# Block 0's attention in two halves, the first FFN tiles begun on half 0, and q's second half loaded last

## The chip, the cores and the metric

The kernel runs on one core of one Trainium2 chip. The time is the device time of that core for one launch, in microseconds. Every run told here was in the fast state. The kernel before took 1116.95 us (median of 3 runs, 1115.8 to 1117.8) when the prediction was made.

## The reference, cut to what matters

```python
kv  = np.einsum('bhsd,bhse->bhde', k, v)         # 8 batches, 8 heads, 576 tokens, width 64
out = np.einsum('bhsd,bhde->bhse', q, kv)
rms = np.sqrt(np.mean(out * out, axis=-1, keepdims=True) + 1e-06)
x   = (out / rms * g_norm)                       # -> (4608, 512), fp32
g   = x @ w_gate                                 # 512 x 1536, float64 in the input
silu = g * (1 / (1 + exp(-g)))
out = (silu * (x @ w_val)) @ w_out               # 1536 x 512
```

Linear attention without a mask, a norm per head, then a gated FFN. The weights arrive as float64 and are rounded to float32 on the core.

## The kernel before: the parts that matter

The 4608 tokens go in nine blocks of 512. Block 0 has no work of another block to hide behind: its attention comes first, on an empty TensorE. Its FFN is "plain", with 12 tiles of 128 columns for the gate and 12 for the value, each of four matmuls of 128x512. The eight later blocks are a different algorithm, and keep TensorE full (119.88 us busy of the 120 from 150 to 270 us).

```python
def all(self):                        # block 0's attention
    for i in range(2):
        self.turn_q(i)                # transposes of q; copies on ScalarE and VectorE
    self.kv(range(NS))                # 192 matmuls of 64x64, wait for k and v
    self.product(0)                   # q @ kv of 256 tokens; squares (ScalarE), sums (VectorE)
    self.product(1, (b_psum, c_psum))
    self.root(0, 2)                   # 1/sqrt of both halves: 11 small VectorE instructions
    for i in range(2):
        self.scale(i)                 # two 128x512 multiplies on VectorE
        self.turn_x(i)                # 8 transposes on TensorE, 2 copies with gain on ScalarE
    return self.scaled
...
def plain_up(self, f):                # one tile of gate and value
    ps = []
    for pool, w in ((b_psum, wg), (c_psum, wv)):
        ps.append(pool.tile([P, BLK], F32, name=pool.name[0]))
        for i in range(NS):
            nc.tensor.matmul(ps[-1], lhsT=w[f // 2][:, i, ...], rhs=self.att.x[:, i, :], ...)
    g = ring("s", BLK)
    nc.scalar.activation(out=g, in_=ps[0], func=ACT.Silu)
    mul(nc.vector, self.h[:, f, :], g, ps[1])
...
blocks[0].load(room)                  # q, then k and v
weights(1)                            # load five weight pieces, round piece 0
scaled = blocks[0].all()
...
        for f in range(NF):
            with tc.issue_after(scaled.ins):
                weights(2 * (f + 2))  # round the pieces that tile f + 1 needs
            ffn.plain_up(f)
        ...
        for j in range(NP):
            t2(wv[j][:, 0:2], wv[j][:, 2:4], wg[j][:, 0:2])   # sums of weights for later blocks
```

`issue_after(x)` queues what stands under it behind x. Rounding one weight piece takes two passes on ScalarE (lines L141 and L143) and four instructions on VectorE (L144, L149, L150, L154).

## Time and profile before

| | before |
|---|---|
| time when predicted, median of 3 | 1116.95 us |
| span of the profiled run | 1113.7 us |
| TensorE busy | 1092.4 us |
| last of the four kv groups starts / ends | 16.66 / 18.21 us |
| first transposes of the normed x start (called T here) | 29.98 us |
| down projection starts | 116.77 us |

Two dates carry the whole argument: T, where TensorE ends its long idle, and the start of the down projection, where block 0's up stage ends. From there to the end of the span it is 996.9 us. The difference between the two dates, 86.79 us, is called the stretch below. In a timeline line the first number is the start, the second the length; the bracket gives the idle time before it and what ended it.

### The profile page before, as it was taken

To read this page: it belongs to the slowest core of one execution; us is meant where nothing else is said; L and a number is where in the kernel's file an instruction comes from. 1 tells how busy PE (TensorE), PEld (TensorE's weight loads), DVE (VectorE), ACT (ScalarE), POOL (GpSimd) and SP (SyncE) were. 2 spreads that over 40 slices of the span, in tenths; PEclk is the share of its full clock that TensorE was granted. 3 is DMA by queue.
4 is the path that set the end of the run, shared out by engine and by line. 5 is a ranking of instruction groups with operands and counts; after the bars stand their busy time and mean duration, and the time that the engine had idled before them with its cause. 6 is when DMAs were issued, how large, how long until landed. Compare 5 with 4: busy or idle time off the path is not lost.

```text
span 1113.7 us, 15512 instructions
## 1 busy us (share of the span) xinstructions
PE 1092.4 (98%) x6528; PEld 901.2 (81%) x6528; DVE 444.2 (40%) x759; ACT 272.4 (24%) x460; POOL 401.0 (36%) x320
## 2 busy tenths in 40 slices
PE   5999999999999999999999999999999999999998
PEld 4444548888888888888888888888888888888887
DVE  2999333126322551156113721263124621561221
ACT  2655112222122212222222122221222122222210
POOL 0021003452344334442444334532543345424550
PEclk9999999999999999999999999999999999999999
DMA  9677410310122010300040012101200100000001
GB/s 273 194 221 186 109 54 19 86 39 1 39 51 51 23 38 26 77 23 26 13 102 23 1 39 61 42 22 38 52 19 1 38 1 1 1 30 10 1 1 38
DMA packets 70245, 57.62 MB, mean 52 GB/s; under 512 B 39456, under 2 KB 64032, under 8 KB 70176
## 3 DMA queue, kind: packets, MB, share of 16 engines
q1 hardware_dynamic: 70112, 56.63, 18.9%
q8 instruction: 51, 0.84, 0.3%
q14 instruction: 18, 0.15, 0.0%
q0 software_dynamic: 64, 0.00, 0.0%
HBM read 47.19 MB, written 9.44 MB: 51 GB/s over the span
## 4 chain that ended last, share of the span: by engine, by line
PE 89%; DVE 1%; DMA 0%; issue 0%
PE b L383 45%; PE c L383 22%; PE a L383 11%; PE b L559 4%; PE m L237 2%; PE m L271 2%; PE m L315 1%; PE m L251 1%; PE b L546 0%; PE c L546 0%; DVE u L150 0%; DMA ld<-in_v_dram 0%; DVE wo L154 0%; DVE g L149 0%; PE a L271 0%; DVE u L144 0%
## 5 line engine op out<-in xcount | busy, mean ns | idle before, releaser
L110 POOL TENSOR_TENSOR t<-wg,wv 128x512 f32<-128x512 f32 x96 | 123.9, 1292 | 182.5 <-PE b L383 92.0
L110 POOL TENSOR_TENSOR t<-wv 128x512 f32<-128x512 f32 x48 | 63.9, 1331 | 323.9 <-PE c L383 117.8
L109 DVE TENSOR_TENSOR s<-h 128x256 f32<-128x256 f32 x48 | 20.4, 425 | 307.8 <-POOL h L111 307.8
L110 POOL TENSOR_TENSOR t<-wo 128x512 f32<-128x512 f32 x72 | 91.4, 1269 | 121.5 <-PE c L383 70.6
L383 PE MATMUL b<-x,t 128*128 128x256 f32 x384 | 91.3, 381 | 0.8
L383 PE MATMUL b<-x,wg 128*128 128x256 f32 x384 | 92.0, 382 | 0.0
L109 DVE TENSOR_TENSOR u<-c,u 128x512 f32<-128x512 f32 x96 | 65.9, 687 | 63.1 <-ACT u L425 63.1
L383 PE MATMUL a<-x,wg 128*128 128x256 f32 x384 | 90.9, 379 | 0.0
L383 PE MATMUL c<-xs,t 128*128 128x256 f32 x384 | 90.8, 379 | 0.0
L383 PE MATMUL b<-xs,t 128*128 128x256 f32 x384 | 90.8, 379 | 0.0
L383 PE MATMUL c<-xs,wv 128*128 128x256 f32 x384 | 90.7, 379 | 0.0
L383 PE MATMUL b<-x,wv 128*128 128x256 f32 x384 | 90.7, 379 | 0.0
L383 PE MATMUL b<-t,h 128*128 128x256 f32 x384 | 86.3, 381 | 0.0
L383 PE MATMUL b<-wo,h 128*128 128x256 f32 x384 | 85.8, 379 | 0.0
L398 ACT COPY u<-b 128x512 f32<-128x512 f32 x56 | 32.8, 586 | 214.2 <-PE b L383 214.2
L383 PEld LDWEIGHTS b<-x,t 128*128 128x128 f32 x384 | 72.3, 190 | 12.0 <-issue 2.5
L383 PEld LDWEIGHTS c<-xs,t 128*128 128x128 f32 x384 | 72.9, 190 | 10.3 <-issue 0.4
L383 PEld LDWEIGHTS b<-xs,t 128*128 128x128 f32 x384 | 72.9, 190 | 10.1 <-issue 0.3
L383 PEld LDWEIGHTS b<-x,wv 128*128 128x128 f32 x384 | 73.0, 190 | 9.9
L383 PEld LDWEIGHTS c<-xs,wv 128*128 128x128 f32 x384 | 73.0, 190 | 9.9
L383 PEld LDWEIGHTS a<-x,wg 128*128 128x128 f32 x384 | 73.0, 190 | 9.9
L111 POOL TENSOR_TENSOR h<-s,u 128x512 f32<-128x512 f32 x48 | 60.9, 1269 | 54.7 <-DVE u L109 54.7
(88 smaller groups left out, 1534.5 us busy)
## 6 DMA issues: line engine op xcount, KB each, us to landing
out_dram<-o SPq DMA_DIRECT2D x18, 512.0 KB, 2.8
ld<-in_q_dram SPq DMA_DIRECT2D x32, 256.0 KB, 5.0
ld<-in_k_dram SPq DMA_DIRECT2D x28, 288.0 KB, 4.6
ld<-in_v_dram SPq DMA_DIRECT2D x28, 288.0 KB, 4.1
ld<-in_moe_w_gate_dram SPq DMA_DIRECT2D x12, 512.0 KB, 4.8
ld<-in_moe_w_val_dram SPq DMA_DIRECT2D x12, 512.0 KB, 5.2
ld<-in_moe_w_out_dram SPq DMA_DIRECT2D x12, 512.0 KB, 4.1
h<-in_k_dram SPq DMA_DIRECT2D x4, 288.0 KB, 6.2
```

What stands on the lines that cost most here:

```text
L109: add = lambda e, o, a, b: e.tensor_tensor(out=o, in0=a, in1=b, op=OP.add)
L110: sub = lambda e, o, a, b: e.tensor_tensor(out=o, in0=a, in1=b, op=OP.subtract)
L111: mul = lambda e, o, a, b: e.tensor_tensor(out=o, in0=a, in1=b, op=OP.mult)
L237: nc.tensor.matmul(self.kv_ps[u * D : (u + 1) * D, j, :], lhsT=self.k[j][:, u, c, :], rhs=self.v[j][:, u, c, :], start=(c == 0), stop=(c = ...
L251: nc.tensor.transpose(ps[:, j], self.q[t][:, j], ident)
L271: nc.tensor.matmul(self.ps[i][u][p : p + D, t, j, :], lhsT=self.qt[rows, 2 * i + t, j, p : p + D], rhs=kvs[b % 3][rows, j, :], start=True, ...
L315: nc.tensor.transpose(ps[:, e, t], xt[:, t, j + e], ident)
L383: nc.tensor.matmul(self.ps[name][:, e], lhsT=lhsT, rhs=rhs, start=first and (e, i) == (0, 0), stop=i == self.steps - 1, skip_group_check=True,
L398: nc.scalar.copy(out=self.u2, in_=self.ps["b"])
L559: nc.tensor.matmul(ps, lhsT=self.h[:, f, P * t : P * (t + 1)], rhs=wo[:, f, :], start=(f == 0), stop=(f == NF - 1),)
```

## The change

The intent is to give TensorE half 0's FFN matmuls while half 1 is still being normed, and to have k and v land sooner by loading q's second half after them. The diff, cut to its core:

```diff
 def load(self, room=None):
-    self.load_q()
+    self.load_q(0)
+    if not room:
+        self.load_q(1)
     ... # k and v
+    if room:                          # block 0 only
+        self.load_q(1)
...
-def all(self):
-    for i in range(2):
-        self.turn_q(i)
-    self.kv(range(NS))
-    self.product(0)
-    self.product(1, (b_psum, c_psum))
-    self.root(0, 2)
-    for i in range(2):
-        self.scale(i)
-        self.turn_x(i)
+def first(self):
+    self.turn_q(0)
+    self.kv(range(NS))
+    self.half(0)                      # product, root and scaling of half 0
+    self.turn_q(1, (b_psum, c_psum))
+    self.product(1, (m_psum, a_psum))
+    self.turn_x(0)
+def second(self):
+    self.root(1)
+    self.scale(1)
+    self.turn_x(1)
...
-def plain_up(self, f):
+def plain_up(self, f, halves=(0, 1)): # may do 256 of the 512 columns
...
-scaled = blocks[0].all()
+scaled = blocks[0].first()
...
+            with tc.issue_after(scaled.ins):
+                weights(2)
+            ffn.plain_up(0, (0,))
+            scaled = blocks[0].second()
             for f in range(NF):
                 with tc.issue_after(scaled.ins):
                     weights(2 * (f + 2))
-                ffn.plain_up(f)
+                if f == 1:
+                    ffn.plain_up(1, (0,))
+                    ffn.plain_up(0, (1,))
+                ffn.plain_up(f, (1,)) if f == 1 else ffn.plain_up(f) if f else None
```

> **What bounds the kernel now.** I read the page first: engine busy times, then the chain that ended last.
>
> ```profile
> span 1113.7 us, 15512 instructions
> ...
> PE 1092.4 (98%) x6528; PEld 901.2 (81%) x6528; DVE 444.2 (40%) x759; ACT 272.4 (24%) x460; POOL 401.0 (36%) x320
> ...
> PE 89%; DVE 1%; DMA 0%; issue 0%
> ```
>
> TensorE is busy for 1092.4 of 1113.7 us, so everything that is not TensorE work adds up to 21.3 us. No reordering can win more than that, and 2% of the run is 22.3 us. Where are those 21.3 us? The table by stretches of time (length, then busy time of each engine, clock, DMA share, GB/s):
>
> ```profile
> 4.20:18.00 13.80, 10.39 (x112) 8.40 (x112) 1.38 (x2) 1.17 (x2) 0.00 (x0) 1.00 1.14 268
> 18.00:24.00 6.00, 4.14 (x132) 3.77 (x129) 3.43 (x6) 4.81 (x9) 0.00 (x0) 1.00 1.10 348
> 24.00:30.00 6.00, 0.24 (x8) 0.05 (x2) 4.73 (x16) 1.09 (x2) 0.00 (x0) 1.00 0.71 223
> 30.00:34.00 4.00, 4.00 (x17) 3.59 (x18) 4.00 (x9) 2.37 (x4) 0.00 (x0) 1.00 0.19 54
> 34.00:60.00 26.00, 26.00 (x62) 11.48 (x61) 24.14 (x51) 18.28 (x30) 0.00 (x0) 1.00 0.81 245
> ```
>
> Almost all of it lies before 30 us: 4.2 us before the first data, 3.4 us up to 18, 1.9 up to 24 and 5.8 between 24 and 30. From 30 on TensorE is full. The list of waits in the first 140 us names the causes (total us, times, longest):
>
> ```profile
> PE m L315 <- DVE xt L111: 5.8, 1, 5.8
> ...
> PE m L251 <- DMA ld<-in_q_dram: 4.5, 2, 4.2
> ...
> PE m L237 <- DMA h<-in_v_dram: 2.9, 4, 1.1
> ...
> PE b L271 <- issue: 1.4, 1, 1.4
> ```
>
> Last the timeline of the stretch that the change touches, and of its end (start, length):
>
> ```profile
> 16.66 1.55 PE L237 MATMUL m<-h 96*64 96x64 f32 x24 [0.57 <-DMA h<-in_v_dram]
> 18.67 1.99 PE L271 MATMUL m<-kv,qt 64*64 64x64 f32 x64 [0.46 <-ACT kv L242]
> 24.78 1.28 DVE L281 TENSOR_REDUCE z<-sq 128x8 f32<-128x512 f32 x2 [1.94 <-ACT sq L280]
> 28.34 0.19 DVE L299 SCALAR_TENSOR_TENSOR y<-a,y 128x32 f32<-128x32 f32 x1
> 28.64 1.29 DVE L111 TENSOR_TENSOR xt<-m,y 128x512 f32<-128x512 f32 x2
> 29.98 3.67 PE L315 MATMUL m<-ident,xt 128*128 128x128 f32 x16 [5.76 <-DVE xt L111]
> 33.58 1.16 PE L546 MATMUL b<-x,wg 128*128 128x512 f32 x2
> ...
> 109.60 3.70 PE L546 MATMUL b<-x,wg 128*128 128x512 f32 x8 [0.18 <-ACT s L551]
> ```
>
> So in the kernel before, TensorE idles 5.8 us while VectorE reduces both halves (from 24.78), takes the root of both in eleven small dependent instructions (to 28.5) and scales (to 29.93). At T = 29.98 it starts 16 transposes. They end at 33.6, and the up projection follows with no hole: 192 matmul instructions at 0.429 us (8 in 3.43 us) are 82.4 us, which would end at 115.98. It ends at 116.77, so about 0.8 us is lost near the end, where ScalarE's Silu comes late (the 0.18 us wait above and 0.2 to 0.3 us either side of it).
>
> [...] Dependent small ops (128x32, 0.19 us long) start 0.225 us apart. Independent ones overlap: a 0.42 us operation is followed 0.33 us later by the next. [...] The trace has 1.28 us and the Silu 1.29 us after the load began, so I use 1.28 alone. [...]
>
> **The change, part by part.**
>
> *Loads.* The second half of q (two 256 KB loads) goes behind k and v. In the trace the third and fourth q pieces move the queue from 5.38 to 8.00, 2.62 us. The kv matmuls wait for each v load and those come 2.15 us apart, so all four groups come 2.62 us earlier: the last ends at 15.6 instead of 18.2. Bytes before the first weight stay the same, so that lands at 18.0 as before.
>
> *Product of half 0.* ScalarE's copy of kv takes 0.46 us with its waits: 16.05 to 18.05. Then the moved q transposes (two tiles, about 0.9 us each): 18.9 and 19.8. Product of half 1: about 20.4 to 22.4. Before, this product had a hole of 1.4 us called issue; it may recur.
>
> *VectorE's order up to the scaling of half 0*, read from the built program. It is not simply half 0 first: the scheduler puts the q copy, the rounding of weight piece 0 and half 1's reduces among half 0's root, and interleaves the two roots. Walking it with measured starts: q copy 18.95; the mask of piece 0 at 19.55; two reduces 19.9 to 21.2; then a stop for ScalarE, which has half 0's squares (18.1 to 19.2), the other q copy (19.8 to 20.4) and two 0.57 us passes for piece 0, done 21.55. Clamp 21.6, XOR 22.05, join 22.8, with three small ops among them, to 23.5; two reduces of half 1, 23.5 to 24.85; then 13 small ops of the two roots. Were each to cost the dependent 0.21 us (128x16 in later blocks), 2.7 us; as they alternate between two chains, half of it: 1.4. So the first scaling starts between 26.3 and 27.6, and two scalings take 1.3: T between 27.7 and 28.95. If the issue hole recurs, half 1's reduces move by a microsecond. I take T = 28.3, 1.7 us before the old 29.98. Thus about a microsecond of the 2.6 won on loads is lost in VectorE's queue.
>
> *From T to full TensorE.* Eight transposes, 1.71 us (16 took 3.41). ScalarE copies the first pair at T+1.16 to T+1.85, and then, in its order, comes a pass for weight piece 3 that needs the buffer of piece 1, rounded on VectorE at about T+2.05; only then the second pair's copy, to about T+3.35. Tile 0's gate half begins at T+1.9, runs 0.86 us, stops 0.6 us for that copy and is full from T+3.37. What remains then: 0.86 (rest of gate half) + 1.72 (value half) + 1.71 (half 1's transposes, scaled by about T+3.7, needed at T+5.9) + 78.96 (82.4 less the 3.44 of tile 0's first half) = 83.25. The end of the up stage is T+86.6, against 29.98+86.0 = 115.98 before without late stalls. Starting on half 0 early gives no time by itself, since before the 16 transposes already ran back to back with ScalarE's copies beside them; it costs 0.6 us in the hand-over. Splitting two tiles into 256 columns costs nothing: the Quad matmuls of 256 columns run 24 in 5.18 us, 0.216 each, twice that is 0.432 against 0.429.
>
> *Late stalls.* VectorE is 24.14 of 26 us busy from 34 to 60 and fuller after, so TensorE's lead could be eaten. It has to pay two more multiplies (about 0.5 us more), but the table load moves to about T+3.8, where nobody waits for it; before, it kept VectorE idle 1.39 us at 41. I expect VectorE at least as far ahead as TensorE, and the old 0.8 us of stall roughly halved.
>
> *Sum.* Up stage ends at 28.3 + 86.6 + 0.4 = 115.3, against 116.77: a gain of 1.5 us. Behind it the order of TensorE is the same and it is full, so the gain comes through to the end: 1116.95 - 1.6 = about 1115.3 us, 0.15% less.
>
> **The rivals.**
> (a) The intent works in full: the 2.6 us of the loads plus the old 5.8 us wait filled, 4 to 6 us gained, 1111 to 1113. For it: the idle is real. Against it: the built order puts half 1's reduces and root before half 0's scaling, so little of the wait is filled.
> (b) VectorE and ScalarE become the bound of the up stage: any lead is paid back as waits for Silu or for the multiply near 105 to 116, and the time stays at 1117. For: VectorE was 29.5 of 30 us busy from 60 to 90, and the only late stall is of this kind. Against: [...] VectorE's own stream starts earlier too.
> (c) The hand-over costs more than T gains: late q, the issue hole, the 0.6 us stop, half 1's scaling late. Then 1117 to 1118.5. For: four queues have to mesh. Against: each has a microsecond or two of slack in my walk.
>
> **Range and chances.** T's spread is 27.7 to 29, the hand-over 0 to 1 us, late stalls 0 to 1.2 us, and three runs of before span 2.0 us. That makes 1113.4 to 1117.2. A change of 2% would be 22 us; the gain is bounded by the idle of 21.3 us, of which this touches less than 9. Faster 0.01, same 0.98, slower 0.01.
>
> **What would show it.** The last kv group ends near 15.6; the first transposes of x start at 27.7 to 29 (at 26 or less, rival a); a hole of about half a microsecond after the first gate matmuls; the down projection starts near 115.3. Waits on Silu or the multiply of over 1.5 us after 90 mean rival b. I am wrong if TensorE is idle for longer than a microsecond after T, or if the kv groups don't come earlier.

The load of 1.28 us in the prediction is ScalarE's table load ahead of the first Silu (L551): it starts at 38.53 us, the Silu at 39.82.

## The result, and the profile after

The changed kernel took 1113.94 us (median of 6 runs, 1113.71 to 1115.68); the kernel before, beside it on the same chip, 1116.32 us (6 runs, 1115.74 to 1117.8). The ratio is 0.9979, with a 95% interval of 0.9967 to 0.9992. A ratio here is the mean time of one kernel's fast runs over that of the other's fast runs of the same rounds, so it is not quite the ratio of the medians quoted. It is a gain of 0.2%, well inside 2%.

The page of the changed kernel, its span, busy times and chain:

```profile
span 1112.1 us, 15596 instructions
...
PE 1091.3 (98%) x6560; PEld 906.8 (82%) x6560; DVE 444.6 (40%) x772; ACT 272.8 (25%) x462; POOL 399.6 (36%) x320
...
PE 97%; DMA 1%; DVE 1%; SPq 0%; issue 0%; ACT 0%
```

The span is 1.6 us shorter: TensorE's busy time fell by 1.1 us (1092.4 to 1091.3), its idle time by 0.5. Filled idle is thus the smaller part of it. The table by stretches of time (busy time of TensorE, weight load, VectorE, ScalarE, GpSimd; then the clock) says where VectorE changed:

```profile
18.00:24.00 6.00, 3.92 (x109) 3.28 (x104) 3.96 (x9) 4.61 (x9) 0.00 (x0) 1.00 1.09 350
24.00:30.00 6.00, 1.73 (x8) 1.57 (x8) 6.00 (x27) 2.00 (x4) 0.00 (x0) 0.72 0.78 240
30.00:34.00 4.00, 4.00 (x11) 3.14 (x11) 3.85 (x11) 3.34 (x6) 0.00 (x0) 0.56 0.47 137
```

VectorE is busy for all 6.00 us from 24 to 30, where it had 4.73 before. And the clock column reads 0.72 and 0.56, where the row of before read 1.00 (why it did is told below). TensorE's timeline at the hand-over and at the end of the up stage (line numbers have shifted: L318 was L315, L556 was L546, L569 was L559):

```profile
14.97 1.55 PE L239 MATMUL m<-h 96*64 96x64 f32 x24 [0.65 <-DMA h<-in_v_dram]
...
28.27 1.94 PE L318 MATMUL m<-ident,xt 128*128 128x128 f32 x8 [5.44 <-DVE xt L111]
30.14 3.64 PE L556 MATMUL b<-x,wg 128*128 128x256 f32 x8
33.62 1.89 PE L556 MATMUL c<-x,wv 128*128 128x256 f32 x8
35.34 1.04 PE L318 MATMUL m<-ident,xt 128*128 128x128 f32 x8
...
115.25 10.46 PE L569 MATMUL b<-wo,h 128*128 128x512 f32 x24
```

T is 28.27, 1.71 us earlier; the down projection starts at 115.25, 1.52 earlier. The idle before T is still 5.44 us: the wait did not go away, it ended sooner. The eight gate matmuls take 3.48 us from their start to that of the value half, the same eight for the value half 1.72 us. Eight transposes take 1.87 us at T and 0.88 us at 35.34. That is one and the same instruction at half speed and at full speed.

VectorE around the first scaling:

```profile
20.04 0.69 DVE L258 COPY qt<-b 128x512 f32<-128x512 f32 x1 [14.14 <-PE b L254]
...
24.11 0.68 DVE L284 TENSOR_REDUCE z<-sq 128x8 f32<-128x512 f32 x1
...
24.79 0.68 DVE L284 TENSOR_REDUCE z<-sq 128x8 f32<-128x512 f32 x1
...
26.84 1.28 DVE L111 TENSOR_TENSOR xt<-m,y 128x512 f32<-128x512 f32 x2
...
30.65 0.69 DVE L111 TENSOR_TENSOR xt<-m,y 128x512 f32<-128x512 f32 x1
```

Half 1's two reduces come 0.7 us sooner than before, without the 1.94 us stop that stood ahead of them; in the stop's place VectorE copies q's moved half and rounds piece 0. Half 0 is scaled 1.4 us after the reduces end, where it was 2.6 us when the whole root of both halves lay between. That makes 1.8 us for the first scaling (28.64 to 26.84). Half 1's scaling follows 3.8 us later; before, it was right behind half 0's.

Was the kernel before at half speed too, at its T? Its clock row reads 1.00. Its durations say yes. Eight of its transposes later in the run:

```profile
155.05 1.04 PE L315 MATMUL m<-ident,xt 128*128 128x128 f32 x8
```

So 16 would take about 1.8 us; at T they took 3.60 (29.98 to 33.58). The row's 1.00 has a plain reason: the clock records kept with this trace begin at 33.69 us, and where there is none the row counts 1.00 (in all the traces here the first record is one of a full clock). In the change they begin at 19.86 (1.00), fall to 0.50 from 26.68 to 33.51, and read 1.00 from there. So the two kernels differ: the change lost its full clock in the idle, the kernel before had not yet reached it. Half 1's product shows the same before any long idle: 0.31 us for one of its matmuls in the kernel before, 0.22 in the change (medians). At a start, where durations of the same instruction differ so much, believe these.

Last, the late stall of before. GpSimd's and VectorE's lines behind it, from two timelines:

```profile
104.01 3.40 POOL L110 TENSOR_TENSOR t<-wg,wv 128x512 f32<-128x512 f32 x2
```

```profile
106.21 1.48 DVE L149 TENSOR_SCALAR g<-ld 128x512 uint32<-128x512 uint32 x1
```

L149 takes 0.42 us elsewhere. While GpSimd made the first weight differences for the later blocks, at 102 to 107 us, three VectorE instructions took 1.16, 1.76 and 1.48 us in place of 0.68, 0.68 and 0.42. VectorE fell behind, Silu came late and the three tiles from 105.83 us on came 0.65 us late in all (0.34, 0.21 and 0.10); the rest of the 0.8 us that the prediction puts here, 0.14, was lost in the first tile, at the slow clock. GpSimd's own instructions are longer there as well: the two from 104.01 us take 3.40 us together, where one takes 1.27 to 1.28 us between 173 and 200 us. At 102 to 107 us, then, both engines ran slower; what slows them no run shows. In the changed kernel GpSimd does the same work at 90 to 96 and 108 to 113 us, three VectorE instructions are stretched just as much (1.16, 1.77 and 1.48 us), and TensorE waits for nothing: the stretching alone does not stall it.

### The profile page after: what moved, and what is told of

It is laid out like the page before. It is cut to its first block, busy times and chain, and to the rows that moved or that the text cites. A ratio compares the mean times of both kernels' runs of the same rounds, so it can differ in the third digit from the quotient of the medians.

```text
span 1112.1 us, 15596 instructions
## 1 busy us (share of the span) xinstructions
PE 1091.3 (98%) x6560; PEld 906.8 (82%) x6560; DVE 444.6 (40%) x772; ACT 272.8 (25%) x462; POOL 399.6 (36%) x320
## 4 chain that ended last, share of the span: by engine, by line
PE 97%; DMA 1%; DVE 1%; SPq 0%; issue 0%; ACT 0%
PE b L388 45%; PE c L388 23%; PE a L388 11%; PE b L556 4%; PE c L556 4%; PE b L569 4%; PE m L239 2%; PE m L274 2%; PE m L318 2%; PE m L254 1%; DMA h<-in_v_dram 1%; SPq L217 0%; DMA ld<-in_v_dram 0%; DVE z L284 0%; PE a L274 0%
## 5 line engine op out<-in xcount | busy, mean ns | idle before, releaser
L110 POOL TENSOR_TENSOR t<-wg,wv 128x512 f32<-128x512 f32 x96 | 124.2, 1294 | 182.4 <-PE b L388 91.8
L110 POOL TENSOR_TENSOR t<-wv 128x512 f32<-128x512 f32 x48 | 62.3, 1299 | 323.6 <-PE b L388 112.8
L109 DVE TENSOR_TENSOR s<-h 128x256 f32<-128x256 f32 x48 | 20.4, 425 | 308.0 <-POOL h L111 308.0
L110 POOL TENSOR_TENSOR t<-wo 128x512 f32<-128x512 f32 x72 | 91.4, 1269 | 121.7 <-PE c L388 70.6
L109 DVE TENSOR_TENSOR u<-c,u 128x512 f32<-128x512 f32 x96 | 65.9, 687 | 63.1 <-ACT u L430 63.1
```

The lines of the kernel that those rows point to most:

```text
L109: add = lambda e, o, a, b: e.tensor_tensor(out=o, in0=a, in1=b, op=OP.add)
L110: sub = lambda e, o, a, b: e.tensor_tensor(out=o, in0=a, in1=b, op=OP.subtract)
```

## The experiments

Twelve runs, of eleven kernels (q_early ran twice). All gave correct results. Their T, stretch and times:

| kernel | T | down projection | stretch | median (range), runs | ratio to before, 95% |
|---|---|---|---|---|---|
| before (first) | 29.98 | 116.77 | 86.79 | 1116.32 (1115.74 to 1117.8), 6 | |
| the change | 28.27 | 115.25 | 86.98 | 1113.94 (1113.71 to 1115.68), 6 | 0.9979 (0.9967 to 0.9992) |
| q_early | 28.18 | 114.64 | 86.46 | 1114.20 (1112.98 to 1114.65), 5 | 0.9982 (0.9970 to 0.9995) |
| q_early_again | 28.56 | 115.42 | 86.86 | 1114.31 (1113.92 to 1116.09), 5 | 0.9991 (0.9977 to 1.0004) |
| before_q_last | 29.92 | 116.63 | 86.71 | 1115.19 (1114.34 to 1115.99), 5 | 0.9994 (0.9980 to 1.0007) |
| no_split | 29.74 | 119.53 | 89.79 | 1118.04 (1116.77 to 1118.48), 5 | 1.0016 (1.0003 to 1.0028) |
| no_split_warm | 28.37 | 118.56 | 90.19 | 1117.18 (1116.05 to 1117.78), 4 | 1.0005 (0.9991 to 1.0020) |
| warm | 29.08 | 116.02 | 86.94 | 1114.31 (1113.19 to 1114.75), 5 | 0.9982 (0.9970 to 0.9995) |
| warm_long | 28.87 | 114.42 | 85.55 | 1113.27 (1112.82 to 1117.55), 6 | 0.9982 (0.9968 to 0.9995) |
| q_early_warm | 29.87 | 115.32 | 85.45 | 1116.50 (1115.14 to 1117.31), 4 | 1.0000 (0.9987 to 1.0013) |
| before_warm | 30.58 | 117.45 | 86.87 | 1115.93 (1115.59 to 1116.52), 4 | 0.9997 (0.9982 to 1.0011) |
| w0_late | 27.27 | 116.97 | 89.70 | 1115.59 (1115.12 to 1116.69), 5 | 0.9994 (0.9982 to 1.0006) |
| both_late | 26.04 | 117.43 | 91.39 | 1115.29 (1115.13 to 1116.00), 5 | 0.9992 (0.9980 to 1.0004) |
| before_t2_late | 30.57 | 117.33 | 86.76 | 1117.02 (1116.77 to 1117.29), 5 | 1.0006 (0.9994 to 1.0018) |

The profile is of one run, the medians of several. The medians of before in these batches were 1115.86 to 1116.36. One and the same sequence of loads lands up to 0.8 us apart in different runs, and T moves with it by as much, so a T is good to about 0.8 us and the medians tell more than one trace.

### Do the loads matter? q_early, before_q_last, q_early_again

q_early is the change with q's second half loaded where it was.

```diff
     self.load_q(0)
-    if not room:
-        self.load_q(1)
+    self.load_q(1)
     ... # k and v
-    if room:
-        self.load_q(1)
```

> The changed kernel with q's second half loaded beside the first again, so only the order of work is changed. If the earlier k and v loads are what moves the start: the last kv group ends near 18.2 us instead of 16.5, the first transposes of x start 1.5 to 1.7 us later than 28.27, near 29.9, and the time is 1115.0 to 1116. Rival, VectorE's queue alone sets that start: it stays within 0.5 us of 28.3 and the time at 1114.

The last kv group and T in its timeline:

```profile
17.19 1.55 PE L235 MATMUL m<-h 96*64 96x64 f32 x24 [0.72 <-DMA h<-in_v_dram]
...
28.18 1.97 PE L314 MATMUL m<-ident,xt 128*128 128x128 f32 x8 [3.98 <-DVE xt L111]
```

The kv groups are 2.2 us later than in the change, and T is the same. In both kernels VectorE scales half 0 at 26.84 us. So the change's load order is not needed for T's gain. before_q_last is the other half of the question: the kernel before, with the change's load order and the q transposes of half 1 behind half 0's product, and nothing else.

```diff
 def all(self):
-    for i in range(2):
-        self.turn_q(i)
+    self.turn_q(0)
     self.kv(range(NS))
     self.product(0)
+    self.turn_q(1, (b_psum, c_psum))
     self.product(1, (b_psum, c_psum))
```

(and `load` as in the change)

> The kernel before with only the load order changed (q's second half after k and v, its transposes after half 0's product), both halves still normed together. If the loads are the whole gain: the first transposes of x start near 28.3 and the time is within 0.5 us of the changed kernel, 1114. If TensorE's slow clock in the first microseconds after its idle decides, the 16 transposes of x, 0.21 us each while slow, fill the slow stretch and the gain is under 1 us: 1115.3 to 1116.3.

```profile
15.49 1.55 PE L240 MATMUL m<-h 96*64 96x64 f32 x24 [0.70 <-DMA h<-in_v_dram]
...
29.92 3.65 PE L319 MATMUL m<-ident,xt 128*128 128x128 f32 x16 [7.11 <-DVE xt L111]
```

The last kv group is 1.2 us earlier than in the kernel before and T has not moved; TensorE only idles longer, 7.11 us. The interval of its time includes the time of before. The load order alone gives nothing that shows.

That does not make T deaf to the loads. In the change VectorE's first work after the loads is the copy of q's second half, at 20.04 us. It waits for the moved transposes (18.89), and these stand behind half 0's product, which waits for k and v. With q last, half 0's scaling starts 11.9 to 12.3 us after the last kv group starts (the change, no_split, no_split_warm, warm, warm_long), and 13.0 in before_q_last, where both halves go through the root first. With q in front it is 9.7 to 10.5 us (q_early, q_early_again, q_early_warm) and 11.7 to 12.0 (before, before_warm, before_t2_late). So moving q lets k and v come about 2 us earlier and lengthens what follows by about as much, and half 0 first shortens it, by 0.7 to 1.1 us with q last and by 1.2 to 2.3 with q in front. Because a later kernel with q in front, q_early_warm below, missed, q_early ran once more, unchanged, on another chip:

> The kernel of q_early once more, unchanged, since q_early_warm missed: there the last kv group came 0.8 us later than in q_early and the first scaling 1.3 us later, and the time was that of the kernel before. Theory (the order of q's loads is worth nothing that shows; q_early_warm was slow for its fillers and for a late load in block 1): median 1113.5 to 1115.0, first scaling between 26.8 and 28.2, stretch from the first transposes to the down projection 86.2 to 87.0 us. Rival (with q's second half in front, the start hangs on the kv loads, and q_early was lucky): first scaling at 28.2 or later and a median of 1115.3 or more.

It scaled half 0 at 27.21 us and took 1114.31 us: the theory holds. This trace is another whose clock records begin late, at 33.54 us. The row reads 1.00 throughout, and yet the gate half took as long as in the change:

```profile
30.45 3.50 PE L552 MATMUL b<-x,wg 128*128 128x256 f32 x8
```

### What is the split of the FFN worth? no_split, no_split_warm

no_split keeps half 0 first in the attention, but the tiles whole, so that no FFN matmul can start before half 1 is turned.

```diff
-            ffn.plain_up(0, (0,))
             scaled = blocks[0].second()
             for f in range(NF):
                 ...
-                if f == 1:
-                    ffn.plain_up(1, (0,))
-                    ffn.plain_up(0, (1,))
-                ffn.plain_up(f, (1,)) if f == 1 else ffn.plain_up(f) if f else None
+                ffn.plain_up(f)
```

> The changed kernel with the two tiles of the FFN whole again, both halves of the attention still in two steps. If starting tile 0 on half 0 is worth what it does in the slow stretch (8 matmuls in place of 8 transposes): 0.8 to 1.5 us slower than the changed kernel, 1114.8 to 1115.4. Rival (my prediction's sum, the split gives no time by itself): within 0.4 us of 1113.9.

It took 1118.04 us, slower than both, and 4.1 us slower than the change, more than either expectation. TensorE waited 1.87 us between the two groups of transposes, and ran at half speed until 38.7 us. Of the 4.3 us by which its down projection starts later in the profiled run, 1.5 are a later T (its last kv group came 1.2 us later), 2.8 the stretch. As the slow clock was mixed into this, the same kernel ran with 56 matmuls of no use ahead of T, to keep the clock up:

```diff
 self.product(1, (m_psum, a_psum))
+warm = c_psum.tile([P, NS, P], F32, name="c")
+with tc.issue_after(self.last_mm.ins):          # the last matmul of product(1)
+    for w in range(56):
+        nc.tensor.transpose(warm[:, w % NS], ident, ident)
 self.turn_x(0)
```

> The change without the division of the FFN's tiles, as in no_split, with 56 matmuls of no use between half 1's product and the transposes, so that the clock is full as in warm_long. Theory (half 0's matmuls hide half 1's scaling and transposes, whatever the clock does): TensorE still idles 1 to 2 us between the two groups of transposes, and the stretch from the first transposes to the down projection is 87.5 to 88.5 us against warm_long's 85.55, so the median is 1115.0 to 1116.0. Rival (no_split lost its 4 us to the slow clock alone): the stretch is 85.5 to 86 us and the median within 0.5 us of warm_long's 1113.3.

```profile
28.37 1.06 PE L318 MATMUL m<-ident,xt 128*128 128x128 f32 x8 [0.21 <-DVE xt L111]
32.10 1.97 PE L318 MATMUL m<-ident,xt 128*128 128x128 f32 x8 [2.66 <-DVE xt L111]
```

Half 0's transposes run at full speed, 1.06 us. Then TensorE idles 2.66 us for half 1's scaling, more than the 1 to 2 us I expected; the clock falls in that idle, and half 1's eight transposes take 1.97 us. The stretch of 90.19 us is worse than the 87.5 to 88.5 expected. The rival, that no_split lost only to the clock, falls: the idle is there with a full clock before it. But the 4.6 us by which it trails warm_long are not the idle alone; they hold a slow clock as well (1.97 us for eight transposes in place of 1.06), which came in this idle. In the changed order, then, half 0's FFN matmuls are what pays: they fill the time until half 1 is scaled, and the clock is full again at 33.5 us in place of 38.7 in no_split.

### Is it the clock? warm, warm_long, before_warm, q_early_warm

The change with 30 such matmuls ahead of T (without the issue_after):

```diff
 self.product(1, (m_psum, a_psum))
+warm = c_psum.tile([P, NS, P], F32, name="c")
+for w in range(30):
+    nc.tensor.transpose(warm[:, w % NS], ident, ident)
 self.turn_x(0)
```

> The changed kernel with 30 transposes of the identity into an unused PSUM tile put into TensorE's 5.4 us of idle (same results). If the clock that falls to 0.5 at 26.7 us costs the time: the clock stays at 1.00, the first eight matmuls of tile 0 take about 2.3 us with their wait instead of 3.5, and the up stage ends 1.0 to 1.3 us earlier: 1112.7 to 1113. Rival, VectorE is the bound of this stretch: TensorE waits for it instead, the time stays at 1113.9.

The 30 ended at 26.7 us, TensorE idled 2.37 us, and the clock fell all the same at 30.1 us: the gate half took 3.46 us. So this run did not test the question. (Its transposes at T, before the fall, took 1.06 us for eight.) warm_long has 50 (`range(50)`), nothing else:

> The changed kernel with 50 filler transposes in place of 30, so that TensorE is busy until half 0 is scaled (30 ended 2.4 us early and the clock fell all the same). If the slow clock costs the time: the clock stays at 1.00 from 24 to 36 us, the eight transposes take 0.9 us, the first eight matmuls under 2.6 us with their wait, and the stretch from the first x transposes to the end of the up stage falls from 87.0 to about 85.3 us; time about 1112.5. Rival, VectorE and ScalarE bound the stretch: it stays above 86.6 us and the time at 1114.

```profile
28.87 1.06 PE L318 MATMUL m<-ident,xt 128*128 128x128 f32 x8 [1.16 <-DVE xt L111]
30.27 2.00 PE L559 MATMUL b<-x,wg 128*128 128x256 f32 x8 [0.34 <-ACT x L319]
```

Now the gate half takes 2.00 us in place of 3.64, and the stretch is 85.55 us, 1.43 less than the change's. The slow clock costs the change about 1.4 us; q_early_warm below, with 85.45 us against q_early's 86.46, shows 1.0. The median, 1113.27 us, is the lowest of all, but one of its six runs took 1117.55, and its ratio to before, 0.9982, is no better than the change's own 0.9979. It is not shown to beat the change.

Is the clock alone enough, without the change? before_warm puts 28 such matmuls behind `self.product(1, (b_psum, c_psum))` in the kernel before:

> The kernel before, with 28 matmuls that compute nothing of use between half 1's product and the first transposes of x, so that the clock is not slow at the hand-over. Theory (the change's gain is VectorE scaling half 0 before half 1; the clock matters only when TensorE is the bound of the start): T stays at about 30.0, the 16 transposes take 1.8 us instead of 3.4, but the up stage then waits for VectorE's rounding of weight pieces 2 and 3, so that the down projection starts at 116.0 to 116.8 and the median falls by 0.5 us at most, to 1115.8 to 1116.4. Rival (the clock at the hand-over is worth its full 1.5 us in any kernel): the down projection starts at 115.0 to 115.4 and the median is 1114.6 to 1115.0.

```profile
30.58 2.29 PE L315 MATMUL m<-ident,xt 128*128 128x128 f32 x16 [2.60 <-DVE xt L111]
33.20 1.13 PE L549 MATMUL b<-x,wg 128*128 128x512 f32 x2 [0.34 <-ACT x L316]
...
35.86 2.84 PE L549 MATMUL b<-x,wg 128*128 128x512 f32 x6 [0.42 <-DVE wg L154]
```

The 16 transposes take 2.29 us in place of 3.67, and TensorE then waits, first for ScalarE's copy, then for VectorE's rounding of a weight piece (L154). The stretch is 86.87 us against 86.79: all of it is given back. The median of 1115.93 us is within the expectation of the theory; the date of 117.45 us is not (116.0 to 116.8), because T itself was 0.6 us later in this run. In the kernel before, a full clock is worth nothing that shows, since VectorE is the next bound.

q_early_warm has q in front and 40 such matmuls, tied behind half 1's product with the issue_after of above:

> The change with q's second half loaded first again, as in q_early, and 40 matmuls of no use after half 1's product. Theory (load order gives nothing, the clock costs the change some 1.4 us): T about 28.2 to 28.8, the clock full from there on, the stretch to the down projection 85.3 to 85.8 us, median 1112.8 to 1113.4, like warm_long. Rival (the loads' order does matter once the clock no longer hides it): T 29.5 or later, median 1114 or more.

This missed: 1116.50 us. The stretch of 85.45 us is as the theory said. But T was 29.87: the last kv group came 0.8 us later than in q_early, half 1's product stood still for 1.69 us (1.45 in q_early, 1.72 in q_early_again), and the 40 matmuls ended at 30.04, after the scaling. And 3.3 us more went in block 1, where no part of the edit lies:

```profile
131.69 0.92 PE L235 MATMUL m<-ld 96*64 96x64 f32 x24 [2.15 <-DMA ld<-in_v_dram]
...
133.23 3.48 PE L569 MATMUL b<-wo,h 128*128 128x512 f32 x4
```

TensorE's wait for a load of v was 1.6 us longer than in the other traces, and the four matmuls after it took 3.48 us in place of 1.88: the clock records read 0.50 from 133.03 to 136.45 us. Its other runs without a profile took 1115.14 to 1117.18 us, so part of the miss is the kernel's own, and how much is open. q_early_again, with the same loads and without these matmuls, did not show it.

### What bounds the start? w0_late, both_late

If half 0 is what VectorE should do first, why let weight piece 0 and half 1's reduces go ahead of it? w0_late only loads the first pieces at that point and rounds piece 0 after half 0's scaling:

```diff
 blocks[0].load(room)
-weights(1)
+while loaded < 5:
+    load_w(*pieces[loaded])
+    loaded += 1
 scaled = blocks[0].first()
```

> The changed kernel with weight piece 0 rounded behind half 0's scaling instead of among its root. The first x transposes should start near 26.1 us, 2 us earlier. If that start sets the end: the down projection starts 1 to 2 us earlier, 1112 to 1113. Rival, VectorE's whole work up to piece 1 and half 1's scaling is the bound and only its order changed: TensorE waits later instead, for piece 0, piece 1 or half 1, and the time stays within 0.5 us of 1114.

both_late also puts half 1's product and its sums behind that scaling:

```diff
-self.product(1, (m_psum, a_psum))
+with tc.issue_after(self.scaled.ins):
+    self.product(1, (m_psum, a_psum))
```

> As the run before, and half 1's two reduces also behind half 0's scaling. First x transposes near 25.5 us. Same rival: half 1's transposes then start later than 33 us and TensorE idles before them, time within 0.5 us of the run before.

The timeline of both_late:

```profile
26.04 1.94 PE L318 MATMUL m<-ident,xt 128*128 128x128 f32 x8 [3.13 <-DVE xt L111]
29.77 3.75 PE L557 MATMUL b<-x,wg 128*128 128x256 f32 x8 [1.79 <-DVE wg L154]
```

T came 1.0 and 2.2 us earlier than in the change, and the down projection 1.7 and 2.2 us later; the medians, 1115.59 and 1115.29 us, are above the change's. Both theories of w0_late expected less, 1114.5 us at most; both_late is within 0.5 us of w0_late, as its rival said. T was earlier than in the change, but 1.2 and 0.5 us later than expected. TensorE gets x early and then waits for piece 0 (1.19 us in w0_late, 1.79 here) and for later pieces. VectorE has to do the q copy, two halves and two weight pieces before TensorE can run on; these two reorderings move the wait and do not shorten it.

### Is the late stall's end part of the gain? before_t2_late

The kernel before, with the weight sums for later blocks behind the last multiply of the up stage, so that GpSimd's differences start later. The sums are VectorE's own work, so VectorE is relieved of them as well:

```diff
+            with tc.issue_after(ffn.last_mul.ins):
             for j in range(NP):
                 t2(wv[j][:, 0:2], wv[j][:, 2:4], wg[j][:, 0:2])
```

> The kernel before with the sums of the weight tiles for the later blocks queued behind VectorE's last multiply of the up stage, so that GpSimd's first work cannot fall beside VectorE near 102 us. If the 0.8 us lost late in the up stage comes from that: no wait for Silu after 100 us, the stretch from the first x transposes to the down projection falls from 86.8 to 86.0 us and the time by 0.8 to about 1115.2. Rival, VectorE's pile of weights alone makes the late stalls: they stay, 1116.

The stall is gone: every later tile starts 3.43 us after the one before. So the stall comes from the sums of the weights. Whether from GpSimd beside VectorE or from VectorE's own sums (L109 at 101.30 and L110 at 109.49 us in before, 0.68 us each), this edit does not part: it moved both. The time is 1117.02 us and the stretch 86.76, the same as before's, because in this run the clock was slow until about 35.5 us, and the first tiles lost as much as the stall had cost. One more microsecond went in block 1, where the moved sums now run beside GpSimd (3.42 us for two, in place of 1.28) and TensorE waits 1.38 us for a copy of q. What the stall is worth in the time is therefore not shown; in the profiled run of before it is 0.65 us.

## Why the prediction was right or wrong

The time (1115.3 predicted, 1113.94 measured), the range and "within 2%" were right, and so was the date of the end of the up stage, 115.3 against 115.25. The gain was forecast at 1.6 us; the medians show 2.4, and the interval of the ratio leaves 0.9 to 3.7. The sum was better than its terms, and its hit is in part luck. Term by term, from the trace of the change:

| term of the sum | predicted, us | measured, us |
|---|---|---|
| T | 28.3 | 28.27 |
| T to the first gate matmul | 1.9 | 1.87 |
| gate half of tile 0, with its stop | 0.86 + 0.6 + 0.86 = 2.3 | 3.48 |
| its value half | 1.72 | 1.72 |
| half 1's transposes | 1.71 | 0.88 |
| the rest, with late stalls | 78.96 + 0.4 | 79.03 |

**T.** The date is right; the reason is not. The prediction had the loads win 2.6 us and VectorE's queue lose "about a microsecond" of it. The kv groups did come earlier, the last ending at 16.52 in place of the 15.6 predicted (they came 2.2 to 2.3 us apart, not 2.15), 1.7 us before the old 18.21. But q_early gets the same T without that, and before_q_last gets none of it with it. What the loads win is lost in the moved work of q, which now stands between k and v and VectorE. What moved T is the order on VectorE. Before, it stopped for 1.94 us for half 1's squares, and then took both halves through the root before scaling half 0. Now half 0's root begins before half 1's squares are there, and the two chains of small instructions alternate. That walk of the queue was right: 14 small instructions lie between 25.38 and 26.84 us, 1.46 us, where I had estimated 13 in 1.4. Its dates were not: q's copy came at 20.04 in place of 18.95 and half 1's reduces at 24.11 in place of 23.5, as k and v were 0.9 us later than predicted. That T fell on 28.3 is luck: I had taken the middle between 1.4 and 2.7 us for the small instructions, and the excess paid for the late start.

**The hand-over.** The step that failed is "it costs 0.6 us in the hand-over", with its cause: "stops 0.6 us for that copy". ScalarE's second copy did end at T + 3.3, as walked. TensorE had no such stop, because at half speed it had not yet come to the matmul that needs it (four matmuls from 30.14 at 0.43 us each end at 31.9, the copy at 31.58). In warm_long, at full clock, ScalarE did both copies in one go, so the predicted stop was not tested there. What happened in its place is the slow clock: 3.48 us for the gate half, 1.2 more than predicted. The prediction also took half 1's transposes at the slow speed, 1.71 us, without seeing that this was a slow speed; they took 0.88. The two errors cancel almost, which is why the date is right. The evidence lay in the trace of before: the same transposes at 0.42 us of length early and 0.27 late. In the change TensorE idled 5.44 us before T, and the clock records read 0.50 from 26.68 us and 1.00 again from 33.51; the other traces do not tie the fall to the length of the idle so simply (see the last section). I had looked at the clock row of before alone, which said 1.00 for want of records.

**"Starting on half 0 early gives no time by itself."** Against the kernel before this is right: there the 16 transposes run back to back. Counting the slow clock, the start even loses: it lengthens the change's first transposes by 0.99 us and its gate half by 1.76, 2.75 together, where before paid 1.84 in its transposes and 0.14 in its first tile. (Not all of the 2.75 can be won back: with the clock full, warm_long waits elsewhere and is 1.43 us better.) But within the change it is wrong to call it worth nothing. Scaling half 0 first makes half 1 come 3.8 us later, and without the split that is lost: no_split and no_split_warm are slower than the change by 4.1 and 3.2 us in their medians. Half 0 first pays only with the split.

**Late stalls.** Predicted halved, 0.4, from an old 0.8; there were none (under 0.1), and the old one was 0.65. So the sum of the changes in the profiled runs is: T -1.71, late stall -0.6, slow clock +0.8 (2.75 less 1.98), together about -1.5, against -1.52 measured at the down projection. No wait was turned into a new one after that; the 996.9 us from there to the end of the span did not change.

**The rivals.** Rival (a), the intent in full, did not happen, for the reason given: VectorE has too much ahead of half 0. The two reorderings of VectorE that were tried, w0_late and both_late, did not get it either. Rival (b), lead paid back late, did not happen: no wait of TensorE stands in the changed trace between 35 us and the down projection. Rival (c) was half right: the hand-over cost more than I gave it, by another mechanism. Three readings of the prediction were loose. Its last sum takes off 1.6 us where its own terms give 1.5. Of the 21.3 us without TensorE work, 15.3 lie before 30 us, which is not "almost all": 4.6 come after the last matmul, at the end of the span. And they are no firm bound, since TensorE's busy time itself fell by 1.1 us. That the two halves of a tile share one PSUM tile made no wait that shows: TensorE's only wait listed from 27 to 117 us of the changed trace is the 5.44 us before T.

**What stays open.** The medians differ by 2.4 us, the two profiled spans by 1.6. The runs of before scatter by 2 us, and its profiled run (1115.45 us) was faster than the six timed ones. Loads that land up to 0.8 us apart and the length of the slow clock differ from run to run, and I think that they make this scatter, but no run took them apart. What made q_early_warm slow beyond what its trace shows is open too, and so is the load of v that came late there.

## What to carry to other kernels

Before you fill a wait, ask which engine's queue ends it: here k and v came 1.7 us earlier and nothing followed, because the work of q that was moved behind them took as long, and the gain in T came from VectorE's order. After a long idle compare the duration of the same matmul early and late before you believe a clock of 1.00, for the records may begin late (at 33.69 us in the kernel before) and the first microseconds may run at half speed (16 transposes took 3.67 us there, 2.29 in before_warm), and an earlier start may only buy slow matmuls (3.48 us for the change's gate half, 2.00 in warm_long). And take a change's parts in pairs: half 0 first lost 2.1 us without the split (1118.04 against 1115.92 for the kernel before in that batch), and gained 2.4 with it.

## What the traces show beside the change

- The length of TensorE's idle does not decide whether the clock falls. It fell after 5.44 us in the change, but also with shorter idles, 2.37 us in warm (eight matmuls then took 3.46 us in place of 2.00) and 2.66 us in no_split_warm, and stayed full over one of 2.60 us in before_warm. What parts them, worked out from the clock records of the 14 traces: its changes lie 3.41 us or multiples of that apart (26.68 and 33.51 us in the change are 6.83 apart), and if the time from the first record on is cut into stretches of 3.41 us, a full clock fell after every one in which TensorE had been busy for 1.57 us or less and after none with 1.61 us or more (fell: 0 us busy in the change, 1.00 in q_early, 1.05 in warm, 1.27 in no_split_warm, 1.57 in no_split; stayed: 1.61 in before_warm, 1.90 in before_q_last, 2.06 in the change). This is a count over these traces; no run set the busy time on purpose to test it.
- The transposes run at both speeds. The fp32 transposes against the identity here, which the trace lists as matmuls, took 1.94 us for eight at half clock and 1.04 to 1.06 us at full clock, and with 50 of them ahead of T the clock stayed full in warm_long (1.00 from 20 to 42 us).
- The clock records of a trace need not reach back to its start. They begin at 33.69 us in the kernel before and at 33.54 us in q_early_again; the row reads 1.00 before that, while 16 transposes take 3.67 us and eight matmuls 3.50.
- Short instructions of two independent chains on VectorE that alternate start about 0.10 us apart (128x16; 12 steps from 25.50 to 26.75 us in the change), against 0.21 us in one dependent chain (128x16; 146.71 to 148.81 us in the kernel before).
- The table load of ScalarE took 1.28 us in the kernel before, and the Silu started 1.29 us after the load began: nothing else shows between the two.
